# Row maxima moved from a matrix product to VectorE's pass over the scores, attention times values in 128x64 tiles, and a new order

## The chip, the core and the metric

The kernel runs on one NeuronCore of a Trainium2 chip. The metric is the device time of one execution in microseconds. The core has a matrix engine (TensorE, PE in the rows; its weight loads stand apart as PEld), three engines for elementwise work (VectorE is DVE, ScalarE is ACT, GpSimd is POOL) and SyncE (SP), which issues the transfers. Each engine takes its own instructions in the order in which they were written, and waits for others by semaphores. TensorE's results land in PSUM, which has eight banks of 128 partitions by 512 numbers of four bytes.

## The reference

A retention layer feeds a mixture of four attention experts. What matters of it:

```
q, k, v: (4, 8, 768, 64)      # batch, heads, positions, width
state = gamma * state + outer(k_t, v_t);   y_t = q_t . state / 8
x = y, heads side by side: (4, 768, 512)
logits = x @ w_gate;  w = softmax of the best two of four logits
for e in range(4):
    qe, ke, ve = x @ wq[e], x @ wk[e], x @ wv[e]           # 768 x 64
    scores = qe @ ke.T / 8, masked above the diagonal
    a = exp(scores - max of each row), each row divided by its sum
    out += (w of e, where e is among the best two) * (a @ ve @ wo[e])
```

## The kernel before, in words

Work is cut into 8 groups j of 384 positions, two for each batch entry: an even j is the first half of the 768 positions, an odd j the second. Retention runs in chunks of 128 positions (functions `h1` and `h2`: products of 64x64 tiles, lines 479, 483, 538 and 544); after each half chunk VectorE scales the state out of PSUM (`sblk`, line 493), and the next half chunk's products need that. `proj` makes queries and keys of a pair p of experts (two pairs, line 595), `vgate` makes values and gate logits (line 614), `mpass` makes scores once in the layout that has a row's maximum along the free axis, and VectorE takes the maxima (lines 692, 706, 726). `mrow` transposes the maxima on TensorE (line 757), ScalarE copies them negated into `mt` (line 759), a transfer writes them to DRAM as `md` (line 761), and two more read them back as two rows `mr` (line 770).

`score(j, p, kb)` then makes the scores transposed, keys on the partitions, for block kb of 128 keys and both experts e of the pair. An even j has three blocks, of width w = 384, 256 and 128 queries; an odd j has six, of 384 four times, then 256 and 128. Numbers are split in a high and a low part, so that three products make a score; a fourth product, of a matrix `oner` that has a single row of ones in each half with `mr`, adds the negated maximum. The four steps alternate between the two experts, each on one half of the array (shape 64x128), and each expert has a PSUM bank. ScalarE takes the exponential of each bank into `pt` (line 856), GpSimd masks diagonal blocks (line 860) and adds up the denominators (lines 869, 876).

```
steps = [(kk[x].t, qq[y].t, ko) for x, y in ((0, 0), (0, 1), (1, 0))] + ([] if sub else [(oner, m.t, 0)])
...
if sub:
    for e in range(2):
        op("DVE", dve_c(w), lambda e=e: nc.vector.tensor_tensor(pt.t[:, e, q0:], sb[e].t[:, :w], m.t[:, e, q0:], op=OP.add), ...)
    op("ACT", act_c(2 * w), lambda: nc.scalar.activation(pt.t[:, :, q0:], pt.t[:, :, q0:], AF.Exp, scale=isc), ...)
```

`sub` is true where j is in the list `SUB`, which is empty before. In a group of that list `mrow` reads `md` back with one transfer that spreads the 768 maxima over all 128 partitions (tile `mb`, 384 KB, line 764), where the two rows of `mr` were 1.5 KB each.

`av(j, p, kbs)` multiplies `pt` with the values (line 895), in full four-byte numbers, each product as two instructions. With `AVT` = 4 the 128 keys of a block are cut in two halves, so that four 64x64 tiles work at a time and two PSUM banks take the halves; `osum` copies one bank out with ScalarE (line 913) and adds the other with VectorE (line 915). With `AVT` = 2 a product goes over all 128 keys in two 128x64 tiles and one bank, and there is nothing to add. `norm_a`, `norm_b` and `norm_last` divide by the sums, `wout` and `wend` multiply with wo (lines 1023, 1059). `norm_last` has the one product of shape 128x64 that the kernel before runs (line 994).

Nothing in the program text is run in the order of its loops. All steps are recorded, and the string `ORDER`, a list of the numbers of the steps, sets the order in which they are written out, on all engines at once; buffers are handed out in that order too. Scores, products and everything else take their banks from seven shared PSUM tiles `ps`; the exponentials go to `NPT` tiles `pt`.

Of the kernel before, what the change touches and what calls it, by code (L numbers as in the profile page):

```python
# [28 lines left out]
SUB = ()  # L29
NQ = 4  # L30
IDLE = (2, 4)
AVT = 4
TURN = 1
NPT = 12
# [209 lines left out]
def tile_retention_moe_attention(  # L244
# [578 lines left out]
    def score(j, p, kb):  # L823
# [7 lines left out]
        w = HS - q0  # L831
        sub = j in SUB
        sb = [Buf(PB) for _ in range(2)]
# [515 lines left out]
```

## Time and profile before

| | us |
|---|---|
| median of three runs (328.75 to 330.71) | 328.85 |
| the profiled execution | 329.46 |
| its span, from the first to the last instruction | 327.70 |
| TensorE busy in the span | 317.7 |
| VectorE, GpSimd, ScalarE busy | 181.0, 167.7, 131.6 |

The rows come from the one profiled execution; 1.76 us of its time lie outside the span. A row of a timeline has the start, the length, the engine, the line and the tiles written and read. A row of the chain of waits, in order of time, has start, length, engine and line: the pieces follow each other without a gap, so a piece's length is the time by which that work moved the end. A busy TensorE is a TensorE with matmuls in flight, not one at its peak.

### The profile page before, as it was taken

What the parts mean: (1) busy time and instruction counts of PE and PEld (TensorE: products, weight loads), DVE (VectorE), ACT (ScalarE), POOL (GpSimd) and SP (SyncE); (2) the same over time, 40 slices, a digit from 0 to 9 for tenths busy, and PEclk for the clock granted to TensorE, in tenths of its full rate; (3) what the DMA queues carried; (4) which work ended last, traced back from release to release, by engine and by line L of the source; (5) the groups of instructions that cost most, each with busy time, mean ns of one, the idle gap of its engine ahead of it and who ended that gap; (6) DMA issues with size and microseconds to landing.
All of it is one profiled execution on the core that took longest, in us unless ns stands there. A gap on an engine that the chain in (4) does not pass through costs nothing.

```text
span 327.7 us, 12383 instructions
## 1 busy us (share of the span) xinstructions
PE 317.7 (97%) x5348; PEld 267.0 (81%) x5348; DVE 181.0 (55%) x506; ACT 131.6 (40%) x352; POOL 167.7 (51%) x192
## 2 busy tenths in 40 slices
PE   7869999999999999999999999999999999999995
PEld 4769999989987869888898778998798679786674
DVE  4634577677637334466555436366753145786953
ACT  1324222334443532345244362254275424457432
POOL 3534542244729993357419677067149921643800
PEclk9969999999999999999999999999999999999998
DMA  7984566244430640438012225200130002111022
GB/s 233 361 300 162 185 237 196 76 148 171 143 113 5 248 172 10 136 106 294 11 50 67 99 68 194 99 26 33 23 106 33 3 10 91 56 66 56 3 99 96
DMA packets 15911, 37.59 MB, mean 115 GB/s; under 512 B 2048, under 2 KB 6256, under 8 KB 15856
## 3 DMA queue, kind: packets, MB, share of 16 engines
q1 hardware_dynamic: 15856, 36.79, 32.9%
q8 instruction: 42, 0.69, 0.8%
q14 instruction: 13, 0.11, 0.1%
HBM read 29.99 MB, written 6.79 MB: 112 GB/s over the span
## 4 chain that ended last, share of the span: by engine, by line
PE 93%; DMA 2%; DVE 1%; issue 1%; SPq 1%; ACT 0%; DVEq 0%
PE ps L595 21%; PE ps L839 14%; PE ps L895 11%; PE ps L614 11%; PE ps L1023 11%; PE ps_st L479 6%; PE ps L692 5%; PE ps L544 5%; PE ps L538 2%; PE ps L483 2%; DMA ot<-in_wvg_dram 2%; PE ps L931 2%; PE ps L978 1%; PE ps L757 1%; PE ps L994 1%
## 5 line engine op out<-in xcount | busy, mean ns | idle before, releaser
L856 ACT ACTIVATE pt<-ps 128x384 f32<-128x384 f32 (+2 forms) x144 | 52.0, 421 | 22.6 <-PE ps L839 18.7
L433 POOL TENSOR_TENSOR qd<-qkT_t,tabs 128x512 f32<-128x512 f32 (+1 forms) x23 | 28.0, 1218 | 52.3 <-PE ps L483 31.4
L595 PE MATMUL ps<-xh,qk_hi 128*128 128x384 f32 x128 | 44.8, 350 | 0.0
L595 PE MATMUL ps<-xh,qk_lo 128*128 128x384 f32 x128 | 43.1, 337 | 0.0
L595 PE MATMUL ps<-xl,qk_hi 128*128 128x384 f32 x128 | 43.1, 337 | 0.0
L876 POOL TENSOR_TENSOR ac<-ac,pt 128x256 f32<-128x256 f32 (+2 forms) x32 | 40.2, 1259 | 1.4
L860 POOL TENSOR_SCALAR_AFFINE_SELECT pt<-pt 128x256 f32<-128x256 f32 x48 | 20.8, 445 | 39.2 <-ACT pt L856 39.1
L895 PE MATMUL ps<-pt,vt 64*64 64x384 f32 (+2 forms) x576 | 40.8, 417 | 0.0
L726 DVE CUSTOM_DVE_ANT_0 scr<-ps,cmask 128x128 bf16<-128x128 f32 (+3 forms) x64 | 29.3, 486 | 20.1 <-PE ps L692 20.1
L493 DVE TENSOR_TENSOR sblk<-ps_st,tabs 128x256 f32<-128x256 f32 x44 | 18.5, 420 | 32.8 <-PE ps_st L479 32.7
L895 PEld LDWEIGHTS ps<-pt,vt 64*64 64x64 f32 x576 | 20.3, 133 | 15.9 <-issue 12.4
L544 PE MATMUL ps<-qkT_t 64*64 64x64 f32 x768 | 27.2, 219 | 3.7 <-issue 3.2
L479 PE MATMUL ps_st<-kv_t 64*64 64x64 f32 x704 | 30.3, 225 | 0.3 <-DVE kv_t L418 0.2
L483 PE MATMUL ps<-qd,sblk 64*64 64x64 f32 x704 | 30.1, 225 | 0.0
L479 PEld LDWEIGHTS ps_st<-kv_t 64*64 64x64 f32 x704 | 25.7, 138 | 5.2 <-issue 3.7
L614 PE MATMUL ps<-vg_hi,xh 128*128 128x260 f32 x96 | 29.3, 305 | 0.2 <-ACT xh L506 0.2
L544 PEld LDWEIGHTS ps<-qkT_t 64*64 64x64 f32 x768 | 25.0, 136 | 4.7 <-issue 3.9
L418 POOL TENSOR_TENSOR kv_t<-kv_t,tabs 128x512 f32<-128x512 f32 (+1 forms) x21 | 20.6, 984 | 16.0 <-PE ps_st L479 9.2
L614 PE MATMUL ps<-vg_hi,xl 128*128 128x260 f32 x96 | 27.6, 288 | 0.6 <-DVE xl L509 0.6
L538 PE MATMUL ps<-am,kv_t 64*64 64x64 f32 x768 | 27.6, 222 | 0.0
L614 PE MATMUL ps<-vg_lo,xh 128*128 128x260 f32 x96 | 27.5, 287 | 0.0
L506 ACT ACTIVATE xh<-ps 128x512 fp32r<-128x512 f32 x24 | 14.3, 596 | 31.7 <-PE ps L483 26.0
(136 smaller groups left out, 781.6 us busy)
## 6 DMA issues: line engine op xcount, KB each, us to landing
qkT_t<-in_qkT_dram SPq DMA_DIRECT2D x24, 512.0 KB
kv_t<-in_kv_dram SPq DMA_DIRECT2D x23, 512.0 KB
out_dram<-ot SPq DMA_DIRECT2D x21, 256.0 KB
fe<-fd SPq DMA_DIRECT2D x28, 96.0 KB
pt<-in_wqk_dram SPq DMA_DIRECT2D x4, 256.0 KB
out_dram<-ot SPq DMA_DIRECT2D x6, 128.0 KB
pt<-in_wo_dram SPq DMA_DIRECT2D x2, 256.0 KB
mr<-md SPq DMA_DIRECT2D x28, 1.5 KB
```

The source lines that it names most:

```text
L479: nc.tensor.matmul(ST[b].t[rows(rt), s * D:(s + 1) * D], kvs(m, 0, s)[rows(rt)], kvs(m, 1, s)[rows(rt)], start=c == 0 and s == 0, stop=Fal ...
L483: nc.tensor.matmul(yo(m, rt, s), SB[m % 2][rows(rt), s], LD[g, 2].t[rows(rt), s, m % 2 * SC:(m % 2 + 1) * SC], start=m % 2 == 0 and s == 0 ...
L538: nc.tensor.matmul(yo(2 * g + u, rt, s), kvs(u + 2 * g, 1, s)[rows(rt)], amg.t[rows(rt), u, s], start=g % NC == 0 and u == 0 and s == 0, s ...
L544: nc.tensor.matmul(ps.t[rows(rt), a:a + SC], qb.t[rows(rt), 1, s, t], qb.t[rows(rt), 0, s, t], start=True, stop=True)
L595: nc.tensor.matmul(pb.t[:, :HS], wsl(ww, kt), xx[:, kt], start=n == 0, stop=n == 11)
L614: nc.tensor.matmul(pb.t[:, :NV + E], xx[:, kt, sl], ww[:, kt], start=n == 0, stop=n == 11)
L726: lambda e=e, scr=scr: nc.vector.tensor_tensor_reduce(scr.t[:, :n1], pb[e].t[:, :n1], K["cmask"][:, HS + C - n1:], 1.0, mx0.t[:, e, i:i + ...
L839: nc.tensor.matmul(sb[e].t[:, :w], k[rows(e), o:o + C], q[rows(e), q0:], start=n == 0, stop=n == len(steps) - 1)
L856: lambda e=e: nc.scalar.activation(pt.t[:, e, q0:], sb[e].t[:, :w], AF.Exp, scale=isc),
L876: op(eng, cost, lambda: en.tensor_tensor(ac.t[:, :, q0:], ac.t[:, :, q0:], pt.t[:, :, q0:], op=OP.add), r=[(pt, 0), (pt, 1), (ac, "b")], w ...
L895: nc.tensor.matmul(ob.t[e * 64:e * 64 + 64, q0:HS], VTB[kj].t[rr, ko // C, ee * 64:ee * 64 + 64], PTB[j, p, kb].t[rr, e, q0:], start=kb == ...
L1023: nc.tensor.matmul(wb.t, oo[:, sl], ww[:, p], start=n == 0 and p == 0, stop=n == 2 and p == NP - 1)
```

## The change

Groups 0 to 6 go into `SUB`: their scores lose the fourth product, VectorE adds the negated maxima (from `mb`) as it moves each bank to `pt`, and ScalarE takes one exponential of both experts in place, from SBUF, where it took two from PSUM. Group 7 keeps the product. `AVT` goes to 2, `NPT` to 10, and `ORDER` is another list throughout (1455 steps, 1429 before).

```
-SUB = ()
+SUB = (0, 1, 2, 3, 4, 5, 6)
...
-AVT = 4
+AVT = 2
...
-NPT = 12
+NPT = 10
...
-1 5 22 0 2 4 23 3 6 108 9 87 11 13 12 7 21 14 10 15 28 26 8 24 27 88 89 29 66 25 16 34 30 42 38 35 36 40 37 44 39 41
+1 5 2 13 3 0 4 23 6 9 11 18 7 8 12 17 14 20 28 24 10 26 25 27 15 42 66 29 16 36 19 30 34 44 48 46 38 47 40 39 37 73 41
```

Line numbers of the new program are higher by one. On TensorE, the first product with the values of the run, group 0; `pt` are exponentials, `vt` values, `ps` PSUM banks. Before:

```order
L538 MATMUL ps_152<-am_71,kv_t_67 64x64
L483 MATMUL ps_152<-qd_69,sblk_163 64x64 x8
L479 MATMUL ps_st_154<-kv_t_68 64x64 x8
L895 MATMUL ps_148<-pt_119,vt_96 64x384
L895 MATMUL ps_153<-pt_119,vt_96 64x384
```

and with the change:

```order
L693 MATMUL ps_151<-kh_85,qh_79 128x384
L693 MATMUL ps_150<-kh_85,qh_79 128x384
L896 MATMUL ps_152<-pt_118,vt_100 64x384 x2
L896 MATMUL ps_152<-pt_117,vt_100 64x256 x2
L896 MATMUL ps_152<-pt_126,vt_100 64x128 x2
L896 MATMUL ps_150<-pt_124,vt_100 64x384 x2
L896 MATMUL ps_150<-pt_123,vt_100 64x256 x2
L896 MATMUL ps_150<-pt_125,vt_100 64x128 x2
L840 MATMUL ps_155<-qh_78,kh_84 128x384
```

Before, these products (shape 64x64, two banks) stood behind retention of the same shape; now (shape 128x64, one bank) they stand between products of shape 64x128. Over the whole program neighbouring steps of TensorE differ in shape 140 times before and 178 times now.

On VectorE, near the start: `vg_lo` and `qk_lo` are low parts of weights, `xl` the low part of the first chunk's retention output, `kv_t_1` the second chunk's keys, scaled. Before:

```order
L351 TENSOR_TENSOR vg_lo_156<-ot_1_136,vg_hi_155 128x260
L351 TENSOR_TENSOR vg_lo_156<-ac_1_126,vg_hi_155 128x260
L509 SCALAR_TENSOR_TENSOR xl_0_74<-ps_1_148,xh_0_72 128x4x128
L552 TENSOR_TENSOR am_1_71<-ps_2_149,am_169 128x512
L493 TENSOR_TENSOR sblk_0_162<-ps_st_0_154,tabs_171 128x256
L418 TENSOR_TENSOR kv_t_1_67<-kv_t_1_67,tabs_171 128x512
```

and with the change:

```order
L510 SCALAR_TENSOR_TENSOR xl_0_74<-ps_1_150,xh_0_72 128x4x128
L352 TENSOR_TENSOR vg_lo_158<-ot_1_138,vg_hi_157 128x260
L352 TENSOR_TENSOR vg_lo_158<-ac_1_128,vg_hi_157 128x260
L553 TENSOR_TENSOR am_1_71<-ps_2_151,am_171 128x512
L1174 MEMSET ones_166 128x1
L352 TENSOR_TENSOR qk_lo_160<-pt_0_117,qk_hi_159 128x512
L494 TENSOR_TENSOR sblk_0_164<-ps_st_0_156,tabs_173 128x256
L419 TENSOR_TENSOR kv_t_1_67<-kv_t_1_67,tabs_173 128x512
```

Both parts of `vg_lo`, which stood ahead of `xl`, and a `qk_lo` now stand between `xl` and the scaling of `kv_t_1`.

On VectorE, in the scores of group 1, the first with six blocks. A stretch of the program before, where the scores leave VectorE nothing to do:

```order
L552 TENSOR_TENSOR am_71<-ps_149,am 128x512
L706 TENSOR_REDUCE mx_0_107<-ps_147 128x1
L706 TENSOR_REDUCE mx_0_107<-ps_151 128x1
L601 TENSOR_TENSOR kl_93<-ps_152,kh_88 128x384
L509 SCALAR_TENSOR_TENSOR xl_75<-ps_153,xh_73 128x4x128
L493 TENSOR_TENSOR sblk_162<-ps_st_154,tabs 128x256
```

and with the change:

```order
L553 TENSOR_TENSOR am_70<-ps_151,am 128x512
L494 TENSOR_TENSOR sblk_165<-ps_st_156,tabs 128x256
L849 TENSOR_TENSOR pt_122<-ps_155,mb_96 128x384
L849 TENSOR_TENSOR pt_122<-ps_152,mb_96 128x384
L602 TENSOR_TENSOR kl_89<-ps_149,kh_84 128x384
L510 SCALAR_TENSOR_TENSOR xl_75<-ps_150,xh_73 128x4x128
L553 TENSOR_TENSOR am_71<-ps_153,am 128x512
L849 TENSOR_TENSOR pt_118<-ps_152,mb_96 128x256
L849 TENSOR_TENSOR pt_117<-ps_154,mb_96 128x128
L494 TENSOR_TENSOR sblk_164<-ps_st_156,tabs 128x256
```

The additions (line 849) stand among the steps that retention waits for, `am` and `sblk`.

## Rows read from the trace of the kernel before

**Rows 1.** The page: busy time of the engines (us, share of the span, instructions), and the chain that ended last by engine.

```profile
PE 317.7 (97%) x5348; PEld 267.0 (81%) x5348; DVE 181.0 (55%) x506; ACT 131.6 (40%) x352; POOL 167.7 (51%) x192
PE 93%; DMA 2%; DVE 1%; issue 1%; SPq 1%; ACT 0%; DVEq 0%
```

**Rows 2.** Waits of TensorE, longest first: what waited, for whom, us in total, times, the longest.

```profile
PE ps L544 <- issue: 3.2, 1, 3.2
PE ps L614 <- DVE xl L509: 0.6, 1, 0.6
PE ps L750 <- DVE mz L745: 0.3, 1, 0.3
```

**Rows 3.** Timeline of TensorE late in the run: steps of a score (each row a pair of instructions, one for each expert) at widths 128, 384 and 256; `mr,oner` is the fourth.

```profile
298.05 0.27 PE L839 MATMUL ps<-mr,oner 64*128 64x128 f32 x2
298.16 0.39 PE L839 MATMUL ps<-qh,kh 64*128 64x384 f32 x2
...
299.44 0.34 PE L839 MATMUL ps<-mr,oner 64*128 64x384 f32 x2
299.62 0.35 PE L839 MATMUL ps<-qh,kh 64*128 64x384 f32 x2
...
304.70 0.28 PE L839 MATMUL ps<-qh,kl 64*128 64x256 f32 x2
304.82 0.28 PE L839 MATMUL ps<-mr,oner 64*128 64x256 f32 x2
```

**Rows 4.** The chain of waits in order of time, six whole steps: two of line 595 (12 products of shape 128x128), two of line 1023 (6 of that shape), two of line 895 (two blocks, shape 64x64). In the first of each two the step ahead has the same shape (lines 614, 595, 483), in the second another (lines 692, 692, 839: 64x128).

```profile
127.75 2.09 PE ps L595 x12
98.97 2.30 PE ps L595 x12
209.53 1.40 PE ps L1023 x6
236.01 1.59 PE ps L1023 x6
191.72 1.29 PE ps L895 x16
117.95 1.45 PE ps L895 x16
```

**Rows 5.** The chain of waits: two steps of line 994 (128x64, width 128, two experts each) and, right behind, two blocks of line 895 (64x64, width 128, two experts each). Then the weight loader's idle time ahead of line 895.

```profile
316.64 0.58 PE ps L994 x8
317.22 0.60 PE ps L895 x16
PEld ps L895 <- issue: 12.4, 70, 0.4
```

**Rows 6.** Groups of instructions, shapes kept apart: line, engine, operation, out and in, partitions x elements, count, busy us, mean ns of one, idle time before.

```profile
L601 DVE TENSOR_TENSOR ql<-ps,qh 128x384 fp32r<-128x384 f32 x16 | 8.8, 550 | 2.4 <-ACT qh L600 2.4
L493 DVE TENSOR_TENSOR sblk<-ps_st,tabs 128x256 f32<-128x256 f32 x44 | 18.5, 420 | 32.8 <-PE ps_st L479 32.7
L677 DVE COPY wt<-ps 128x128 f32<-128x128 f32 x4 | 1.1, 286 | 3.9 <-PE ps L675 3.8
L915 DVE TENSOR_TENSOR on<-ps,on 128x384 f32<-128x384 f32 x14 | 7.7, 555 | 14.5 <-ACT on L913 13.7 <-PE ps L839 0.7
L856 ACT ACTIVATE pt<-ps 128x384 f32<-128x384 f32 x80 | 35.2, 493 | 9.6 <-PE ps L839 9.1 <-PE ps L692 0.3
L872 ACT ACTIVATE ac<-pt 128x256 f32<-128x256 f32 x8 | 3.3, 407 | 0.0
L351 DVE TENSOR_TENSOR qk_lo<-pt,qk_hi 128x512 fp32r<-128x512 f32 x2 | 2.1, 1034 | 2.4 <-ACT qk_hi L350 2.4
```

**Rows 7.** SyncE's timeline around one set of maxima (`md` out, `mr` back) and another.

```profile
57.03 0.33 SPq L761 DMA_DIRECT2D md<-mt  x1
...
58.24 0.54 SPq L770 DMA_DIRECT2D mr<-md  x2
...
157.44 0.28 SPq L761 DMA_DIRECT2D md<-mt  x1
158.67 0.55 SPq L770 DMA_DIRECT2D mr<-md  x2
```

**Rows 8.** The start. First GpSimd's timeline (`wu` is the operand of eight products that warm TensorE up, `ident` a mask), then the chain of waits.

```profile
0.94 0.20 POOL L1144 MEMSET wu<- 128x128 bf16 x1
1.53 0.29 POOL L1150 TENSOR_SCALAR_AFFINE_SELECT ident<-cmask 128x128 f32<-128x128 f32 x1
...
10.26 0.88 DVE vg_lo L351
11.14 0.66 DVE xl L509
12.72 0.72 DVE kv_t L418
16.27 3.19 issue
```

**Rows 9.** Stretches of the start: from and to, length, then busy us (and instructions) of PE, PEld, DVE, ACT, POOL, the granted share of TensorE's clock, the DMA engines' share, GB/s.

```profile
16.00:20.00 4.00, 0.81 (x24) 0.68 (x24) 2.19 (x3) 0.90 (x2) 2.59 (x4) 0.84 0.94 292
20.00:23.00 3.00, 3.00 (x97) 3.00 (x93) 0.42 (x1) 0.00 (x0) 0.00 (x0) 0.50 1.04 414
23.00:27.00 4.00, 4.00 (x34) 3.88 (x30) 2.24 (x4) 1.56 (x4) 3.40 (x3) 0.68 0.36 104
```

103 rows, old and new, of the table ORDER are left out of this document.

## The prediction

> **What bounds the kernel now.** I read the page first: TensorE is busy for 317.7 of 327.7 us and 93% of the chain that ended last is its work, while VectorE is at 55% and ScalarE at 40% [rows 1]. A busy engine need not be a bound one, so I went on to its waits: the longest is one of 3.2 us, the next is 0.6 [rows 2]. The 3.2 us is the "issue" at 16.27 us, near the start [rows 8]; no engine and no transfer ended it, so the profile does not say what it was. From there to the end TensorE waits for nobody by more than a few tenths. So what counts is the sum of TensorE's own steps, plus what the start loses, plus any wait that the change makes.
>
> The sum is made against the profiled execution, 329.46 us (a span of 327.70 and 1.76 outside it). That is 0.6 above the median of 328.85, within the spread of the three runs, so I carry the difference over to the median.
>
> **Removed: the fourth product.** Rows of TensorE's timeline give the price of one pair as the distance to the next pair: 0.11 us at width 128, 0.18 at 384 (0.174 over several in a row), 0.12 at 256 [rows 3]. Groups 0, 2, 4, 6 have, for each of two pairs of experts, one block of each width: 8 of each. Groups 1, 3, 5 have four of 384 and one each of the others: 24, 6, 6. In all 32 x 0.174 + 14 x 0.115 + 14 x 0.11 = 5.6 + 1.6 + 1.5 = 8.7 us. TensorE has no idle time beside it, so all of it is on the path: -8.7 us.
>
> **Moved: the shapes.** A step that follows one of another shape takes longer than the same step behind one of its own: 2.30 against 2.09 us for a projection, 1.59 against 1.40 for an output product, 1.45 against 1.29 for two blocks times values [rows 4]. So a change of shape costs 0.16 to 0.21 us. The values' products ran in the shape of retention, and often stood beside it; in 128x64 they share their shape with almost nothing. Counted in the two orders, 140 changes become 178. 38 x 0.185 = +7.0 us (6.1 to 8.0). No row shows a change between 64x128 and 128x64, the commonest of the new ones; if it were no dearer than half the cheapest seen, 0.08, the term would be +3.0, which I take as the lower bound for the range. What the removal gives, the changes of shape nearly take back.
>
> **Changed: the values' products.** Two steps of the one product that already has shape 128x64, at width 128 and for two experts, take 0.58 us in 8 instructions; two blocks at the same width in 64x64 take 0.60 in 16 [rows 5]. Each moves the same numbers through the array, and the smaller tiles worked side by side. So I take 0 (between -0.02 and +0.02 for two blocks of 128). The instruction count halves, and the weight loader has 12.4 us of idle time ahead of these products, in 70 places [rows 5]; the chain shows matmuls in flight beside it, so I give nothing for that.
>
> **Added on VectorE.** Two additions a score: 64 of 384, 28 of 256, 28 of 128. The nearest rows read PSUM and SBUF as these do or have the same size: 0.55, 0.42 and 0.286 us [rows 6]. That is 35.4 + 11.8 + 8.0 = 55 us; the 20 additions of `osum` that go away took 7.7 in the 14 large ones [rows 6] and, at 0.286 each, 1.7 in six small ones. VectorE goes from 181 to about 227 us, 69% of the span. Its cover is TensorE's work; as long as VectorE keeps up, the price is 0. On ScalarE two exponentials of 0.49 us become one over 768 numbers out of SBUF, between the 0.41 that a third of that size takes there [rows 6] and three times as much, 1.22. The engine is at 40%: 0 either way.
>
> **What waits behind the additions.** An addition waits for the broadcast of the maxima, and VectorE's queue is in order: behind it stand `sblk` and `am`, which retention on TensorE waits for, and the two banks of the score stay taken. Adding up TensorE's steps in the new order at the durations of the rows above, I find between `mrow` and the end of the first score that needs it 2.6 and 3.3 us at the tightest two of 14 places, 4.1 to 4.9 at four others, and more at the rest. The way of the maxima: 1.2 us from the issue of `md` to that of what reads it back (57.03 to 58.24, 157.44 to 158.67) [rows 7], 0.4 ahead of it for ScalarE's copy, as for the small one in the rows [rows 6], and a landing that no row shows. Estimate for it: another 1.2 like the first, plus 393 KB at the best rate seen, 414 GB/s [rows 9], 0.95 us. In all 3.8 us, say 4. So VectorE stands still for 1.4 and 0.7 us at two places, by TensorE's sum, and has some 30% of free time to catch up in. I take +0.2, with 0 and +5 as ends.
>
> **The start.** Three things move. `wu`, which TensorE's first products need, is set after two masks, so about 0.9 us later (0.94 against the end of `ident`, 1.82) [rows 8]. VectorE's chain to the second chunk's keys ran `vg_lo`, `xl`, ..., `kv_t` without a gap [rows 8]; now both `vg_lo` (0.4 and 0.88) and a `qk_lo` (1.03) [rows 6] stand between `xl` and `kv_t`: +2.3, less 0.4 because `xl` no longer waits for `vg_lo`. So TensorE comes to the second chunk about 2.8 us later. The stall of 3.19 us lies 2.8 us behind that point. If it is tied to the place in TensorE's program, all 2.8 are lost; if it ends at a time of its own, it swallows them. I take half, +1.4. Behind the stall the granted clock falls to 0.50, its lower level of 1.2 GHz, after 0.81 us of work in 4 us; over three stretches that makes 6.8 us at half speed, 3.4 us of work [rows 9]. I leave that as it is; it could go (-3.4) or last as long again (+3.4).
>
> **The end.** TensorE's wait of 0.3 us for the last maxima (`mz`) [rows 2] is covered in the new order by two scores that stand ahead of it: -0.3. Fewer `pt` buffers and one bank instead of two for the values: TensorE waits for neither now [rows 2], 0.
>
> **Sum.** -8.7 + 7.0 + 0.2 + 1.4 - 0.3 = -0.4: 329.1 for the profiled execution, 328.4 us for the median.
>
> **The rivals.** *The changes of shape are cheap, or the start is.* With +3.0 for the shapes and 0 for the start the sum is -5.8; with the shapes as I have them, the start at 0 and the half-speed stretch gone, -5.2. About 323.5 us. For it: the new kind of change was never measured. Against it: three kinds of step agree on 0.16 to 0.21.
>
> *VectorE takes the place of TensorE* (slower). Mechanism: the broadcast lands late, because it queues behind loads of 512 KB (1.3 us each at 414 GB/s) on the same queue. Two such loads ahead make 6.6 us of the 4, and then nine of the 14 places have less lead than that; VectorE stands still for about 2 us at each, and `sblk` and the banks are late. One `sblk` falls due in 7.4 us (44 in the span [rows 6]), and VectorE's free 31% of that, 2.3 us, would cover such a stop if it were spread evenly; beside a run of additions it is not, and I price what TensorE feels at a third of each stop, an estimate: 9 x 0.6 = +5.4, so 333.8 us. It decides from the point where the maxima take more than about 5 us from `mrow` to landing. For it: the additions bunch where the scores are, and a queue in order lets nothing pass. Against it: no wait of TensorE for VectorE over 0.6 us exists now. The Trainium skill points the same way (TensorEngine Tiling (Array Packing), section PSUM Bottleneck): moving results out of PSUM may become the bottleneck, and both ScalarE and VectorE should do it; this change takes the scores from ScalarE, and by that rule the slower case is the likely one. The rows so far put VectorE at 69%, short of it.
>
> *Small matmuls are bound by their count.* If the 12.4 us that the weight loader idles ahead of the values' products were time of the path, halving the instructions would give back half, 6.2 us: 322.2 us. Against it: 0.58 and 0.60 us for 8 and 16 instructions. The Trainium skill has a rule for it (the same page, section Instruction Overhead): about 60 cycles for each matmul whatever its size. By it 288 matmuls fewer would be worth some 7 us, as an estimate from that page, if they ran one behind the other; here four tiles run side by side.
>
> **How the numbers follow.** About 1% (3.3 us) is what a measurement of this kernel tells from no change. The forecast, a swap on TensorE that ends between -2.9 (shapes at 6.1, start and VectorE at 0) and +2.0 (8.0, 2.8, 0.2), 326.0 to 330.9: 55%. The shapes or the start cheap, 323.5: 18%. VectorE, 333.8: 24%. The instruction count, 322.2: 3%. The range is 324.0 to 333.0: the forecast whole, two thirds of the first rival and half of the second. Faster by over 1%, under 325.5: the first and the last rival less 1%, 20%. Slower by over 1%, over 332.2: 24%. Within: the forecast and that 1%, 56%.
>
> **What would show it.** In the profile after: TensorE still at 96% or more with no wait over 1 us behind the start; the steps of a score at 3/4 of their time; the values' products at 1.3 us for two blocks of 384, but 1.45 to 1.5 behind another shape; VectorE near 227 us. The first product of the second chunk (13.4 us now, where `kv_t` ends) [rows 8] near 16.3. Wrong would be: waits of TensorE for `sblk` or for banks behind additions, the additions with idle time ahead that a broadcast ended, or a change into 128x64 that costs 0.1 or 0.3.

## The result, and the profile after

With the change the kernel takes 331.89 us (median of 12 runs, 329.87 to 333.06) where the kernel before takes 329.56 (12 runs): a ratio of 1.0079, 95% interval 1.0054 to 1.0105, so 2.6 us (1.8 to 3.5) slower. The forecast was 0.4 us faster; the time lies inside its range of 324.0 to 333.0, on the other side of no change. The profiled execution took 332.15 us, its span 330.4.

The page after, to be held against [rows 1]:

```profile
PE 316.8 (96%) x4940; PEld 257.8 (78%) x4940; DVE 220.5 (67%) x606; ACT 127.5 (39%) x292; POOL 166.8 (50%) x192
PE 89%; DMA 4%; issue 3%; DVE 1%; POOL 1%; ACT 0%; SPq 0%; DVEq 0%; POOLq 0%
```

TensorE's waits after, longest first, as in [rows 2]:

```profile
PE ps_st L480 <- DVE kv_t L419: 2.4, 1, 2.4
PE ps L1195 <- POOL wu L1145: 1.9, 1, 1.9
PE ps L615 <- POOL vg_lo L352: 1.6, 1, 1.6
PE ps L615 <- issue: 1.4, 1, 1.4
PE ps L545 <- DMA qkT_t<-in_qkT_dram: 1.3, 1, 1.3
```

TensorE's busy time fell by 0.9 us and its idle time grew. All five waits lie in the first 35 us. To split the run in two I use one step as a mark: the fourth product of values and gate logits, which both programs reach with the same steps of TensorE behind them but for one filler. Its first product before, then after:

```profile
42.27 0.39 PE L614 MATMUL ps<-vg_hi,xh 128*128 128x260 f32 x1
```

```profile
46.82 0.39 PE L615 MATMUL ps<-vg_hi,xh 128*128 128x260 f32 x1
```

The start became 4.55 us longer. From the mark to the end of the span it is 285.4 us before and 283.6 after: the rest became 1.8 us shorter. The prediction's terms for the rest make -8.7 + 7.0 + 0.2 - 0.3 = -1.8. So the whole miss lies in the start, which it had at +1.4.

TensorE's timeline after, a step of values and the scores behind it (columns as in [rows 3]):

```profile
107.73 1.51 PE L896 MATMUL ps<-pt,vt 128*64 128x384 f32 x8
109.17 0.45 PE L840 MATMUL ps<-qh,kh 64*128 64x384 f32 x2
...
109.80 0.34 PE L840 MATMUL ps<-qh,kh 64*128 64x384 f32 x2
109.97 0.33 PE L840 MATMUL ps<-ql,kh 64*128 64x384 f32 x2
110.15 0.34 PE L840 MATMUL ps<-qh,kl 64*128 64x384 f32 x2
```

A score is three pairs 0.17 to 0.18 us apart, the fourth is gone. Two blocks of 384 times values take 1.44 us behind another shape (107.73 to 109.17), as in 64x64 [rows 4]: the new shape costs and gains nothing.

VectorE's additions after, groups by width, as in [rows 6]:

```profile
L849 DVE TENSOR_TENSOR pt<-ps,mb 128x384 f32<-128x384 f32 x64 | 32.7, 550 | 6.9 <-DMA mb<-md 3.7 <-PE ps L840 2.9
L849 DVE TENSOR_TENSOR pt<-ps,mb 128x256 f32<-128x256 f32 x28 | 11.1, 416 | 5.6 <-PE ps L840 4.8 <-issue 0.5 <-DMA mb<-md 0.2
L849 DVE TENSOR_TENSOR pt<-ps,mb 128x128 f32<-128x128 f32 x28 | 7.2, 282 | 5.3 <-PE ps L840 3.1 <-DMA mb<-md 2.3
```

And the longest of VectorE's waits for the broadcast, by the view of waits (us in total, times, longest):

```profile
DVE pt L849 <- DMA mb<-md: 6.2, 7, 2.3
```

0.550, 0.416 and 0.282 us against the estimates 0.55, 0.42 and 0.286 [rows 6]. VectorE did stand still for the broadcast, seven times, 6.2 us in all. Behind the longest stop, and only there, TensorE shows a wait (VectorE, then TensorE):

```profile
75.02 0.82 DVE L849 TENSOR_TENSOR pt<-ps,mb 128x128 f32<-128x128 f32 x3 [2.27 <-DMA mb<-md]
75.76 0.41 DVE L494 TENSOR_TENSOR sblk<-ps_st,tabs 128x256 f32<-128x256 f32 x1
...
76.23 0.27 PE L480 MATMUL ps_st<-kv_t 64*64 64x64 f32 x1 [0.18 <-DVE sblk L494]
```

That is 0.18 us. The chain of waits runs through 5.55 us of that broadcast, yet TensorE worked beside all but these 0.18: a piece of the chain is not always the time by which it moved the end.

Where the start went, in four timelines of the profile after (TensorE; ScalarE; VectorE; GpSimd; in brackets the idle time ahead and what ended it):

```profile
6.83 1.97 PE L545 MATMUL ps<-qkT_t 64*64 64x64 f32 x32 [1.31 <-DMA qkT_t<-in_qkT_dram]
...
13.81 0.39 PE L615 MATMUL ps<-vg_hi,xh 128*128 128x260 f32 x1 [0.42 <-ACT xh L507]
15.82 0.39 PE L615 MATMUL ps<-vg_lo,xh 128*128 128x260 f32 x1 [1.62 <-POOL vg_lo L352]
...
20.12 0.37 PE L480 MATMUL ps_st<-kv_t 64*64 64x64 f32 x1 [2.43 <-DVE kv_t L419]
...
10.14 0.73 ACT L351 ACTIVATE vg_hi<-ot 128x260 fp32r<-128x260 f32 x2 [8.06 <-DMA ot<-in_wvg_dram]
13.16 0.60 ACT L507 ACTIVATE xh<-ps 128x512 fp32r<-128x512 f32 x1 [2.29 <-PE ps L484]
13.66 0.72 ACT L351 ACTIVATE vg_hi<-ac 128x260 fp32r<-128x260 f32 x2
...
13.79 0.69 DVE L510 SCALAR_TENSOR_TENSOR xl<-ps,xh 128x512 fp32r<-128x512 f32 x1 [1.47 <-ACT xh L507]
14.40 0.77 DVE L352 TENSOR_TENSOR vg_lo<-ot,vg_hi 128x260 fp32r<-128x260 f32 x1
15.10 0.95 DVE L352 TENSOR_TENSOR vg_lo<-ac,vg_hi 128x260 fp32r<-128x260 f32 x1
15.97 0.68 DVE L553 TENSOR_TENSOR am<-ps,am 128x512 f32<-128x512 f32 x1
16.58 1.81 DVE L352 TENSOR_TENSOR qk_lo<-pt,qk_hi 128x512 fp32r<-128x512 f32 x1
...
18.32 0.41 DVE L494 TENSOR_TENSOR sblk<-ps_st,tabs 128x256 f32<-128x256 f32 x1
18.65 1.41 DVE L419 TENSOR_TENSOR kv_t<-kv_t,tabs 128x512 f32<-128x512 f32 x1
...
16.57 1.28 POOL L434 TENSOR_TENSOR qd<-qkT_t,tabs 128x512 f32<-128x512 f32 x1
17.81 1.71 POOL L352 TENSOR_TENSOR qk_lo<-pt,qk_hi 128x512 fp32r<-128x512 f32 x1
```

The second chunk's first product stands at 20.12 us; before it followed `kv_t` at 13.48 [rows 8]. The delay is 6.6 us, not 2.8. It has two parts. The value step began at 13.81, 10.78 before: 3.0 us, since the first `qkT` landed later (the first real product at 6.83, 4.99 before) and the first products then ran slowly (1.97 us for 32 that took 1.11; what slowed them is open). From there to the second chunk it is 6.3 us, 2.7 before: 3.6 us. VectorE decides there: from `xl` at 13.79 to the end of `kv_t` at 20.06 it has no gap, with both `vg_lo` and a `qk_lo` ahead of `kv_t`. On ScalarE the third and fourth `vg_hi` stand behind `xh`, where before they came ahead of it; GpSimd's `vg_lo` waits for them, and TensorE 1.62 us for that, all inside VectorE's time.

### The profile page after: what moved, and what is told of

Its sections match the earlier page's. It is cut to its first block, busy times and chain, and to the rows that moved or that the text cites. A ratio compares the mean times of both kernels' runs of the same rounds, so it can differ in the third digit from the quotient of the medians.

```text
span 330.4 us, 11560 instructions
## 1 busy us (share of the span) xinstructions
PE 316.8 (96%) x4940; PEld 257.8 (78%) x4940; DVE 220.5 (67%) x606; ACT 127.5 (39%) x292; POOL 166.8 (50%) x192
## 4 chain that ended last, share of the span: by engine, by line
PE 89%; DMA 4%; issue 3%; DVE 1%; POOL 1%; ACT 0%; SPq 0%; DVEq 0%; POOLq 0%
PE ps L596 20%; PE ps L896 12%; PE ps L840 11%; PE ps L1024 11%; PE ps L615 10%; PE ps_st L480 5%; PE ps L693 5%; PE ps L545 5%; PE ps L539 2%; PE ps L484 2%; DMA mb<-md 2%; PE ps L932 2%; DMA qkT_t<-in_qkT_dram 2%; PE ps L979 1%; DMA md<-mt 1%
## 5 line engine op out<-in xcount | busy, mean ns | idle before, releaser
L849 DVE TENSOR_TENSOR pt<-ps,mb 128x384 f32<-128x384 f32 (+2 forms) x120 | 49.2, 456 | 17.8 <-PE ps L840 10.8
L852 ACT ACTIVATE pt<-pt 128x768 f32<-128x768 f32 (+2 forms) x60 | 40.3, 690 | 20.3 <-DVE pt L849 20.1
L896 PE MATMUL ps<-pt,vt 128*64 128x384 f32 (+2 forms) x288 | 41.8, 424 | 0.0
L870 POOL TENSOR_TENSOR ac<-pt,pt 128x512 f32<-128x512 f32 (+1 forms) x14 | 21.3, 1522 | 25.9 <-ACT pt L852 22.3
L480 PEld LDWEIGHTS ps_st<-kv_t 64*64 64x64 f32 x704 | 25.4, 138 | 8.0 <-issue 3.0
L896 PEld LDWEIGHTS ps<-pt,vt 128*64 128x64 f32 x288 | 18.2, 136 | 17.0 <-issue 11.8
L615 PE MATMUL ps<-vg_hi,xh 128*128 128x260 f32 x96 | 28.8, 300 | 1.8 <-issue 1.4
L545 PE MATMUL ps<-qkT_t 64*64 64x64 f32 x768 | 28.4, 227 | 1.5 <-DMA qkT_t<-in_qkT_dram 1.3
L545 PEld LDWEIGHTS ps<-qkT_t 64*64 64x64 f32 x768 | 26.2, 143 | 3.0 <-DMA qkT_t<-in_qkT_dram 2.2
```

Of the source, the lines that this page charges most:

```text
L480: nc.tensor.matmul(ST[b].t[rows(rt), s * D:(s + 1) * D], kvs(m, 0, s)[rows(rt)], kvs(m, 1, s)[rows(rt)], start=c == 0 and s == 0, stop=Fal ...
L545: nc.tensor.matmul(ps.t[rows(rt), a:a + SC], qb.t[rows(rt), 1, s, t], qb.t[rows(rt), 0, s, t], start=True, stop=True)
L615: nc.tensor.matmul(pb.t[:, :NV + E], xx[:, kt, sl], ww[:, kt], start=n == 0, stop=n == 11)
L896: nc.tensor.matmul(ob.t[e * 64:e * 64 + 64, q0:HS], VTB[kj].t[rr, ko // C, ee * 64:ee * 64 + 64], PTB[j, p, kb].t[rr, e, q0:], start=kb == ...
```

## Experiments

Each was timed against the kernel before; times from ratios are ratio times 329.6. First the start, taken from one kernel and put into the other. Both edits are in `ORDER` alone: its first 150 numbers follow the other kernel's sequence of steps, the rest stays.

**The changed kernel with the start of before.**

```diff
-1 5 2 13 3 0 4 23 6 9 11 18 7 8 12 17 14 20 28 24 10 26 25 27 15 42 66 29 16 36 19 30 34 44 48 46 38 47 40 39 37 73 41
+1 5 22 0 2 4 23 3 6 108 9 87 11 13 12 7 21 14 10 15 28 26 8 24 27 88 89 29 66 25 16 34 30 42 38 35 36 40 37 44 39 41 48
...
```

> The changed kernel, with the first 150 steps of the order (up to the gate and value product behind the second half of the first batch entry's chunks, all engines and loads) in the order of the kernel before; the rest as changed. Theory 'start': the profiles show the same stretch of work ending 4.55 us later with the change (46.82 against 42.27 us) and the rest 1.85 us shorter (283.58 against 285.43 us), so this kernel loses nothing at the start: 1.9 us faster than the kernel before (ratio 0.994), about 4.5 under the changed kernel. Rival 'VectorE or the shapes': what costs is spread over the run, and the start's delay is caught up later or would be there anyway: within 1 us of the changed kernel, some 2.5 us slower than before (ratio 1.008).

Measured: 333.25 us, ratio 1.0131 (1.0082 to 1.0179). By the number the theory fell; by the trace it did not. The mark stood at 41.85 us, five earlier than with the change, but at 44.2 us TensorE waited 4.6 us for `ql`:

```profile
PE ps L693 <- DVE ql L602: 4.6, 1, 4.6
```

VectorE was held by the difference of a piece of `wo`, whose load had come to stand behind loads that waited for buffers. The seam between the two orders had made a wait of its own.

**The same without that wait.** ScalarE's copy goes behind the steps that stood after it, VectorE's difference `wo_lo` alike:

```diff
-L351 ACTIVATE wo_hi<-pt 128x512
...
+L351 ACTIVATE wo_hi<-pt 128x512
```

> As e1_start_of_before, with two steps moved back: ScalarE's copy and VectorE's difference of one piece of wo (first needed much later) stand where the kernel before has them, behind the scaling of the next logits, not ahead of a difference ql that TensorE waits for. In e1 its start was restored (the value step that is the marker at 41.85 us, 42.27 before, 46.82 with the change), but then TensorE waited 4.6 us for ql, which stood behind that piece's late load, and ran at half speed for 3.4 us after it. Theory 'start': without that wait 41.9 us of start and 280.5 + 3.1 us of rest, a span of 325.5: 2 us faster than before (ratio 0.993). Rival 'the delay only moves': the rest becomes longer as the start becomes shorter, because the rest of the changed order waits for the same loads or for VectorE: 329 to 333 us (ratio 1.000 to 1.010), with other waits in the place of that for ql.

Measured: 326.96 us, ratio 0.9932 (0.9894 to 0.9970), where the theory said 0.993. With the start of before the rest of the change is a gain: 2.2 us faster than the kernel before, 4.8 faster than the changed kernel. It beats both. (A profile is one execution: this kernel's took 329.84 us, with a stall of 4.33 that is shown below. Its mark stood at 44.09 us; from there to the end it has 283.9 us, as the changed kernel has 283.6.)

**The kernel before with the start of the changed one** (the same edit the other way).

> The kernel before, with the first 150 steps in the order of the changed kernel; nothing else of the change. Theory 'start': the whole loss comes with these steps: 4.5 us slower than the kernel before (ratio 1.014), since no gain stands against it. Rival 'VectorE or the shapes': no slower than 1 us (ratio up to 1.003). My forecast of the start, +1.4 (0 to 2.8), would be a ratio of 1.004 (1.000 to 1.0085).

Measured: 333.02 us, ratio 1.0111 (1.0065 to 1.0156), +3.7 us (2.1 to 5.1). The mark stood at 46.89 us, in the changed kernel at 46.82; the rest was as before. The upper end of my +1.4 lies inside the interval, +1.4 itself doesn't.

**Two parts of the start, in the changed kernel.** On VectorE, then on ScalarE:

```diff
-L510 SCALAR_TENSOR_TENSOR xl_74<-ps_150,xh_72 128x4x128
 L352 TENSOR_TENSOR vg_lo<-ot_138,vg_hi 128x260
 L352 TENSOR_TENSOR vg_lo<-ac_128,vg_hi 128x260
+L510 SCALAR_TENSOR_TENSOR xl_74<-ps_150,xh_72 128x4x128
...
+L494 TENSOR_TENSOR sblk_164<-ps_st_156,tabs 128x256
+L419 TENSOR_TENSOR kv_t_67<-kv_t_67,tabs 128x512
 L352 TENSOR_TENSOR qk_lo<-pt_117,qk_hi 128x512
-L494 TENSOR_TENSOR sblk_164<-ps_st_156,tabs 128x256
-L419 TENSOR_TENSOR kv_t_67<-kv_t_67,tabs 128x512
```

```diff
-L507 ACTIVATE xh_72<-ps_150 128x4x128
 L351 ACTIVATE vg_hi<-ac_127 128x260
 L351 ACTIVATE vg_hi<-ac_128 128x260
+L507 ACTIVATE xh_72<-ps_150 128x4x128
```

> The changed kernel with five steps near the start put as in the kernel before: on ScalarE the third and fourth vg_hi ahead of xh, on VectorE both vg_lo ahead of xl, and the scaling of the second chunk's keys (kv_t) ahead of the first qk_lo. Loads and GpSimd as changed. The first product of the second chunk stood at 20.12 us with the change, 13.48 before. Theory 'VectorE's and ScalarE's order': it comes to about 16.5 us, and 3 to 3.6 of the 4.6 us that the start lost come back: 328.5 us (ratio 0.997). Rival 'the loads': the first real product stays at 6.8 us (5.0 before), half speed until 10 us stays, weights come no earlier; what is gained at the second chunk is lost again at the next wait: within 1 us of the changed kernel (ratio 1.005 to 1.01).

Measured: 330.48 us, ratio 1.0028 (0.9988 to 1.0069): 1.7 us off the changed kernel (0.1 to 3.3 by the two intervals), half of what the theory gave. The second chunk came at 17.26 us, 2.9 earlier, but 2.1 and 1.0 us of "issue" that the waits had covered came out behind it.

One load, on SyncE:

```diff
-L345 DMA ac_127<-in_wvg_dram 128x260
 L380 DMA qkT_t_63<-in_qkT_dram 128x1024
 L384 DMA kv_t_66<-in_kv_dram 128x512
 L380 DMA qkT_t_64<-in_qkT_dram 128x1024
+L345 DMA ac_127<-in_wvg_dram 128x260
```

> The changed kernel with one transfer moved: the piece of wvg that was issued ahead of the first chunk's qkT goes behind the second chunk's qkT. Theory 'loads': the first qkT lands sooner than 6.79 us (4.9 before) by the 0.47 us of an issue and by the time of 133 KB, TensorE starts sooner and reaches full speed sooner: 0.5 to 1.8 us faster than the changed kernel (ratio 1.002 to 1.006). Rival 'VectorE's and ScalarE's order': the second chunk waits for qk_lo and kv_t all the same: no change (ratio 1.008).

Measured: 330.37 us, ratio 1.0027 (0.9989 to 1.0066), also 1.7 us (0.2 to 3.2). The first real product stood at 5.46 us in place of 6.83, the mark at 44.96. This load I had not priced at all.

The two edits together:

> The changed kernel with the edits of e8_after_vector_order and of e9_after_one_load together. Each alone was 1.7 us faster than the changed kernel by its ratio (1.0028 and 1.0027 against 1.0079). Theory 'two independent delays, one ahead of the other on the path': they add up, -3.4 us, ratio 0.997 to 0.998, and what is left to e2_start_mended (0.9932) lies in the rest of the start's order. Rival 'one wait covers the other' (the piece of TensorE's program, "issue", comes when it comes): no more than -2 us in all, ratio 1.002.

Measured: 329.48 us, ratio 0.9999 (0.9973 to 1.0025): 2.6 us off (1.5 to 3.8), between the two theories, and the interval holds both. What the other 2.2 us to the whole start are was not split further.

**The settings one by one, in the old order.** AVT alone:

```diff
-AVT = 4
+AVT = 2
```

> The kernel before with AVT = 2 alone, in its own order, less the 20 additions on VectorE that add up two banks. Neighbouring steps of TensorE differ in shape 150 times, 140 before. By the prediction's terms: 10 x 0.185 = +1.9 us, the values' products themselves 0: ratio 1.0056. Rival 'the shapes are cheap': +0.8 or less. Rival 'small matmuls are bound by their count' (288 instructions fewer): -6.2 + 1.9 = -4.3 us, ratio 0.987.

Measured: 329.37 us, ratio 1.0009 (0.9974 to 1.0043): +0.3 us (-0.9 to 1.4). The instruction count is out: 288 matmuls fewer gave nothing. The +1.9 of my terms lies outside the interval too. Behind the mark its profile is 1.0 us longer than the kernel's before (286.5 against 285.5), where ten changes of shape at the 0.16 found below make 1.6: too small a run to size one.

SUB alone, in the kernel before:

```diff
-SUB = ()
+SUB = (0, 1, 2, 3, 4, 5, 6)
...
-    MB = tag("mb", NQ, [128, 2, HS]) if SUB else None
+    MB = tag("mb", 2, [128, 2, HS]) if SUB else None
```

> The kernel before with SUB = (0, ..., 6) alone, in its own order: the fourth product goes, and each pair of exponentials on ScalarE becomes two additions on VectorE at the same places and one exponential; two mb tiles in place of four. Values' products in 64x64 as before, 140 changes of shape as before. By the prediction's terms: -8.7 + 0.2 = -8.5 us (ratio 0.974). Rival 'VectorE takes the place of TensorE': the additions stand ahead of the steps that retention waits for; by the 9 stops of 0.6 us, +5.4, in all -3.3 us (ratio 0.990), with waits of TensorE for sblk or for the banks of the scores to be seen. If the fourth product is worth only half of what the row spacing says: -4.2.

Measured: 338.01 us, ratio 1.0260 (1.0207 to 1.0314): 8.6 us slower, with some 8.6 us of products gone. VectorE's timeline in one stretch, and the row of TensorE's that ends it:

```profile
82.01 0.55 DVE L848 TENSOR_TENSOR pt<-ps,mb 128x384 f32<-128x384 f32 x1
82.47 0.41 DVE L493 TENSOR_TENSOR sblk<-ps_st,tabs 128x256 f32<-128x256 f32 x1
82.80 0.55 DVE L848 TENSOR_TENSOR pt<-ps,mb 128x384 f32<-128x384 f32 x1
83.27 0.61 DVE L726 CUSTOM_DVE_ANT_0 scr<-ps,cmask,mx 128x384 bf16<-128x384 f32 x1
83.80 0.08 DVE L726 DVE_READ_ACCUMULATOR2_ANT mx<- 128x1 f32 x1
83.80 0.28 DVE L848 TENSOR_TENSOR pt<-ps,mb 128x128 f32<-128x128 f32 x1
84.00 0.61 DVE L726 CUSTOM_DVE_ANT_0 scr<-ps,cmask,mx 128x384 bf16<-128x384 f32 x1
...
84.67 0.33 PE L757 MATMUL ps<-ident,mx 128*128 128x128 f32 x1 [1.22 <-DVE mx L726]
```

And the group of its additions:

```profile
L848 DVE TENSOR_TENSOR pt<-ps,mb 128x384 f32<-128x384 f32 (+2 forms) x120 | 50.4, 455 | 1.7 <-PE ps L839 1.4 <-PE ps L692 0.2
```

The additions stand among the reductions for the maxima (line 726), VectorE works without a gap, and TensorE waits for `mx`. That is one place. Over the run TensorE and its weight loader wait longer for the additions themselves, which empty the banks that the next products write (us in total, times, longest):

```profile
PEld ps L839 <- DVE pt L848: 3.8, 10, 1.4
...
PEld ps L692 <- DVE pt L848: 1.8, 5, 0.6
...
PE ps L757 <- DVE mx L726: 1.2, 1, 1.2
```

For additions the weight loader waits 8.2 us in all. These waits do not add up to the whole loss; how the rest is spread is open. Ahead of its additions VectorE is idle for 1.7 us in all; in the changed kernel, with the same additions in another order, for 17.8:

```profile
L849 DVE TENSOR_TENSOR pt<-ps,mb 128x384 f32<-128x384 f32 (+2 forms) x120 | 49.2, 456 | 17.8 <-PE ps L840 10.8 <-DMA mb<-md 6.2 <-issue 0.5
```

Both settings, old order:

```diff
-SUB = ()
+SUB = (0, 1, 2, 3, 4, 5, 6)
...
-AVT = 4
+AVT = 2
```

> The kernel before with SUB = (0, ..., 6) and AVT = 2, in its own order: the change without its new order (two mb tiles, twelve pt). SUB alone in this order was slower by 2.6% (+8.5 us) where TensorE's sum says -8.3; AVT = 2 alone +0.1%. Theory 'the order makes the room': VectorE's queue has the additions ahead of what TensorE waits for as in e6, so 337 to 340 us (ratio 1.023 to 1.031), and the new order is worth some 10 us against this. Rival 'it was VectorE's load': AVT = 2 takes 20 additions, 9 us, from VectorE, so a sixth of what the additions brought; the loss shrinks by that much or more: 332 to 336 us (ratio 1.007 to 1.02).

Measured: 337.75 us, ratio 1.0254 (1.0215 to 1.0293). VectorE's 9 us less did not help; the order makes the room. The two `mb` tiles in place of four are no rival: in neither trace does an addition wait for `mb`.

**The changed kernel with the fourth product back.**

```diff
-SUB = (0, 1, 2, 3, 4, 5, 6)
+SUB = ()
```

> The changed kernel in its own order and with AVT = 2, but SUB = (): the fourth product is back, VectorE's 120 additions are gone, two exponentials on ScalarE stand where the additions stood. Start as in the changed kernel. By the prediction's terms, additions hidden: +8.5 us on the changed kernel, about 340.4 us (ratio 1.033 to before); the steps of scores grow by 0.15 us at width 384, 0.14 at 256, 0.11 at 128, in all 8.3. Rival 'VectorE takes the place of TensorE': the additions cost something in the changed kernel too, and what they cost comes back here: +3 to +5 us only, 335 to 337 us (ratio 1.017 to 1.024).

Measured: 340.70 us, ratio 1.0326 (1.0268 to 1.0384): 8.8 us over the changed kernel by the medians, 8.1 by the ratios, as the terms had it. In the new order the additions cost the end nothing that shows: the interval leaves some 2 us either way.

**The stall.** The mended kernel with the second value step ahead of it on TensorE:

```diff
+L615 MATMUL ps_150<-vg_hi,xh_72 128x260
...
 L545 MATMUL ps_152<-qkT_t_63 64x64 x16
```

> As e2_start_mended, with the second vgate step (24 instructions of TensorE, 1.4 us) moved ahead of the retention step in which TensorE stands still with "issue" (3.2 us before, 3.4 in e1, 4.3 in e2, 2.9 in e5), and on VectorE the xl that it needs ahead of the scaling of the third chunk's keys. In those four profiles a 16 KB packet of the queue called instruction ends 1.4 us ahead of the end of the stall. Theory 'TensorE waits for the next piece of its program': the piece does not come sooner or later for the work that stands ahead of it, so the 1.4 us of vgate come for nothing: 1.4 us faster than e2 (ratio 0.989), up to 3.4 more where TensorE's clock then does not fall. Rival 'the stall belongs to the step, or VectorE's order decides there': no gain, or a loss of 0.7 us by the later kv_t (ratio 0.993 to 0.996).

Measured: 327.49 us, ratio 0.9951 (0.9922 to 0.9980): no gain on the mended kernel that could be told. The stall itself went, from

```profile
16.77 0.87 PE L545 MATMUL ps<-qkT_t 64*64 64x64 f32 x24
21.98 0.58 PE L545 MATMUL ps<-qkT_t 64*64 64x64 f32 x5 [4.33 <-issue]
```

in the mended kernel to this wait:

```profile
PE ps L545 <- issue: 0.2, 1, 0.2
```

The mark in its profile stood at 41.83 us, against 44.09 in the mended kernel's (whose profile took 329.84 us where its median is 326.96) and 41.85 where the start of before was put in unmended. Waits of 0.6 to 0.7 us for `xh`, `xl` and "issue" stand there now. TensorE's granted clock was at its lower level, 1.2 GHz, from 25.4 to 28.8 us, but that does not explain the time: ten of the twelve executions had a granted clock of 0.998 or more and were no faster. The half of the theory on the stall held, the half on the time fell, and why is open.

## Why the prediction was wrong, step by step

**The fourth product, -8.7.** Right. Scores of the same width between the same neighbours are 0.17, 0.115 and 0.11 us shorter in the two profiles: 32 x 0.17 + 14 x 0.115 + 14 x 0.11 = 8.6, and putting it back cost 8.1 to 8.8.

**The shapes, +7.0.** Right within its range. Fitting all steps behind 50 us of the profile after by their kind and by whether a neighbour has another shape gives 0.16 to 0.17 us for a change; 64x128 to 128x64 and back, which I had no row for, lie at the same value. 38 x 0.165 = 6.3. The lower bound of +3.0 was not needed. So measured, the terms behind the start make -8.6 + 6.3 + 0.2 - 0.3 = -2.4, where the profiles have -1.8; that the forecast's own terms meet it to a tenth is in part luck.

**The values' products, 0,** and the rival of the instruction count: right, and out.

**VectorE and the broadcast, +0.2.** Right for this order: the one wait of TensorE behind a broadcast is 0.18 us, and the fourth product's return shows no price of the additions. The idle time that a broadcast ends ahead of additions, which I named as a sign of being wrong, did show, 6.2 us of it, and meant nothing. The rival was no phantom: in the old order it took some 17 us, three times what it got from me, by another way than mine. I had it wait for the broadcast; there the additions themselves come late, and with them the banks and the maxima. The Trainium skill's sentence (TensorEngine Tiling (Array Packing), section PSUM Bottleneck), that moving results out of PSUM may become the bottleneck once tiling has sped TensorE up, agrees with the old order's +2.6% and not with the new one.

**The start, +1.4 (0 to 2.8).** This step failed. It measured 4.55 us in the profiles and 3.7 (2.1 to 5.1) when put alone into the kernel before. I had one of its two mechanisms, work ahead of the second chunk's keys, and that too small. I did not follow SyncE: a load ahead of the first `qkT`, in a part that lost 3.0 us where I had 0.9 for `wu`. And I took `qk_lo` and `kv_t` at their lengths, 1.03 and 0.72 us; they took 1.81 and 1.41 beside GpSimd (below), so that VectorE's part lost 3.6 us where I had 1.9. ScalarE, where two `vg_hi` had gone behind `xh`, I did not follow either; its delay lay inside VectorE's. `wu` was 0.7 us late and cost nothing that shows, since `qkT` came later still. Of the 6.6 us of delay, 2.1 were swallowed, a third where I took half: behind the second chunk the stall of 3.2 us [rows 8] was not there, and one of 1.4 us came later.

**The clock.** As left in the two profiles: 6.8 us at 1.2 GHz in both, from 18.7 us before and from 16.9 after; such a stretch makes a mean granted clock of 0.99. Over the executions it was not as left. The twelve of the changed kernel have 0.988 to 0.993, 0.9898 on the mean; the 69 of the kernel before that were timed beside the experiments have 0.987 to 1.000, 0.9936 on the mean, 42 of them above 0.992. By the two means the changed kernel loses some 1.3 us more to the clock (0.0038 x 330, an estimate). So a part of the loss at the start is the clock, which I had as even; how the loss splits between it and the waits is open.

**The end, -0.3.** Right: no wait for `mz` is left.

**What would show it.** The first product of the second chunk, named there at 16.3 us, stood at 20.1: the place to look was right, and read at once it tells the miss.

## What to carry to other kernels

When an order is rewritten, cost the start on every queue apart, the loads' and the copying engine's too, and follow each operand of the first products back to its load; behind the start, where one engine is never idle, a sum over that engine's steps came here within some tenths of a per cent. Work moved to an idle engine is free only where the order keeps it from standing ahead of what the bound engine waits for: the same additions cost some 17 us in one order and nothing that shows in another. And when two orders are spliced to test a part, read the trace for the wait that the seam makes before believing the time.

## What the runs showed of the hardware

**TensorE's program comes in pieces, through the transfers.** The page's queue "instruction" carried, before and after:

```profile
q8 instruction: 42, 0.69, 0.8%
```

```profile
q8 instruction: 38, 0.62, 0.8%
```

That is 16 KB a packet, and 0.69 MB over TensorE's 10,696 products and weight loads [rows 1] is 64 bytes each; with 9,880 it is 63. That the packets are TensorE's program is read from this fit and from what follows. Five kernels stop with "issue" behind the same 24th product of the same step, at 16.3 to 17.6 us, and go on 1.37 to 1.44 us after such a packet has ended: before at 18.0 and 19.46, in the mended kernel at 20.5 and 21.98. So the stall begins at a place in the program and ends when the next piece is there; other waits run beside it at no cost. In the changed kernel the 1.4 us of "issue" that end at 34.78 end so too, 1.27 us after a packet. That is the answer to what the prediction left open.

**VectorE waits out GpSimd.** In the profile after `qk_lo` ends 0.54 us after GpSimd's `qd` (16.57 + 1.28 = 17.85, 16.58 + 1.81 = 18.39), and `kv_t` 0.54 after GpSimd's `qk_lo` (19.52, 20.06). Before, and in the kernel with VectorE's order:

```profile
16.10 1.48 DVE L418 TENSOR_TENSOR kv_t<-kv_t,tabs 128x512 f32<-128x512 f32 x1
...
15.77 1.27 POOL L433 TENSOR_TENSOR qd<-qkT_t,tabs 128x512 f32<-128x512 f32 x1 [2.89 <-PE ps L483]
```

```profile
15.84 1.37 DVE L419 TENSOR_TENSOR kv_t<-kv_t,tabs 128x512 f32<-128x512 f32 x1
...
15.37 1.29 POOL L352 TENSOR_TENSOR qk_lo<-pt,qk_hi 128x512 fp32r<-128x512 f32 x1
```

Again 0.54 and 0.55. With nothing beside it such a step takes 0.68 to 0.70. All four of these VectorE steps have both inputs in SBUF, which is the Trainium skill's rule (SBUF — State Buffer, section Summary: rules for kernel authors): VectorE with two SBUF inputs and a GpSimd step that reads SBUF exclude each other for the whole instruction. The trace agrees: `sblk`, with one input in PSUM, took its usual 0.41 us beside GpSimd's `qk_lo` (at 18.32 above).
